# Idle matmuls at the start, eight transposes moved to the tensor engine, and a new written-out order

## The chip, the cores and the metric

The kernel runs on one core of one Trainium2 chip. The metric is the device time of one execution in microseconds (us). A difference is told against the runs of the kernel before on the same chip.

## The reference

Two computations in a row. First a causal attention with a decay ("forgetting attention"), for 8 batches of 8 heads, 576 positions and 64 channels:

```python
scores = (1 / sqrt(D)) * q @ k.T
cum = cumsum(log(clip(f, 1e-4, 1)))               # per head, along the sequence
scores = where(causal, -1e9, scores + cum[i] - cum[j])
attn = exp(scores - rowmax); attn /= attn.sum()
x = attn @ v                                      # x: 4608 tokens x 512
```

Then a bilinear feed-forward network on the 4608 tokens, with 512 channels and 1536 hidden ones:

```python
out = ((x @ w_a) * (x @ w_b)) @ w_out
```

## The kernel before

**Work units.** Heads are worked on in pairs; a pair of one batch is a unit `t` (0 to 31, four units in a batch). The 576 queries of a unit are five blocks (four of 128 and one of 64). For each unit: q and k are loaded, cast to 16 bits and transposed by the tensor engine (`pe_transpose`, tile psT, L285); the scores are made in groups (`qk_group`, tile sc, L417); VectorE adds the decay and takes the row maximum (`do_max` L514 for batch 0, `do_decay` L540 later); ScalarE takes the exponential into P, a 16-bit tile (tiles PA and PB, L567 and L571); VectorE inverts the sums (L581), GpSimd scales P (`do_norm`, L589); P is transposed; the tensor engine multiplies it with v (`do_pv` L631, `do_pv4` L647); VectorE copies the result to xT, the network's input. The network goes through the tokens in pieces of 256, 256, 256, 384 and then 512: 12 steps of psa and psb (`ff_mm`, L914, four matmuls each), a copy by ScalarE (L240), a product by VectorE (L925, tile ht), and pso (L934).

**How P is transposed.** Blocks of P are parts: A0 (six 128x128 blocks, query blocks 0 and 1), A1 (six, query block 2), both joined as A from batch 2 (counting from 0) on, and B (thirteen). For batch 0 (`PEP`) the tensor engine transposes P (`pe_tr`, tile psP, L609) and VectorE or ScalarE copies the result from PSUM (`pe_tr_evict`). For all others SP issues a DMA transpose (`do_tr`). In batches 0 and 1 the transposed A0 and A1 lie in the upper half of xT's storage, so the profile names that transfer xT<-PA. Batches are counted from 1 in the change's own words: its "batch 2" holds the units 4 to 7.

**The decay.** f is loaded, clipped, its logarithm taken on ScalarE and summed up by a scan on VectorE (L187); its high and low 16-bit parts are the tile crow. For batch 0 the decay comes to the scores by extra matmuls on crow; for the units 4 to 7 (`PSPREAD`) it is spread over the rows by a matmul (`spread_mm`, tile scd, L482).

**Weights.** GpSimd issues the loads of w_a and w_b (two row halves, each in a first part of 512 columns and a second part of 1024) and of w_out (L392). Step 0 of the network needs both row halves of the first parts.

**What sets the order.** Every step is an `Op` with a planned engine, duration and dependencies. The planner is not in the file: its result is, as the list `ORDER` of Op numbers, and the string `CHOICE`, which gives the engine of each Op that may run on more than one. The kernel emits the Ops in that order, so each engine's queue, the DMA issues of SP and those of GpSimd among them, is fixed by it. An engine works its queue in order: an instruction that waits holds all those behind it. PSUM and SBUF tiles come from rings (two sc, one pv, three ff).

Of the kernel before, what the change touches and what calls it, by code (L numbers as in the profile page):

```python
# [9 lines left out]
FP32 = mybir.dt.float32  # L10
# [15 lines left out]
def kernel(  # L26
# [11 lines left out]
    nc = tc.nc  # L38
# [32 lines left out]

    def constants():
        make_identity(nc, ident16)
# [130 lines left out]
    o_c = Op("POOL", 4.5, lambda _: constants(), prio=-300)  # L204
# [99 lines left out]
    PEP = tuple(range(1))  # L304

# [372 lines left out]
    def attention(t, base):  # L678
# [12 lines left out]
        if not direct:  # L691
            if t in PSPREAD:
# [340 lines left out]
    for n in cuts:  # L1033
# [3 lines left out]
        0 1 26 20 32 38 3-6 27 28 11 7 2 29 30 12 21 22 8 10 9 13 14 19 33 34 23 24 31 25 18 61 64 35 70 106 15  # L1037
# [7 lines left out]
        178 1739 173 256 174 1741-1743 272 1740 1744 275 265 266 179 273 1745 104 139 276 289 283 282 290 105  # L1045
# [3 lines left out]
        1762-1764 280 287 60 288 221 222 226 484 264 328 385 329 293 150 330 294 472 473 231 1765 334 1766 384  # L1049
        378 339 232 373 1767 1768 379 386 233 194 1769 1771 389 390 340 388 387 485 295 234 1770 1773 341 1774  # L1050
        342 391 392 1775 336 195 1772 1776 274 296 297 393 303 304 474 1777-1779 239 298 475 299 305 1780 338
# [4 lines left out]
        1802 427-429 439 440 435 1804 313 1805 1807 1806 1809 1808 1810 314 424 434 1811 442 441 1812 1813  # L1056
# [4 lines left out]
        528 519-521 529 546 1837 545 413 414 552 1838 530-532 553 547 507 533 514 513 579 676 1786 458 671 460  # L1061
# [6 lines left out]
        608 616 594 636 617-619 614 643 644 620 637 610 684 622 609 596 621 615 1893-1896 638 645 639 646 1898  # L1068
# [10 lines left out]
        1969-1971 798 895 896 816 897 797 1972 787 788 811 794 821 822 1973 823 1974 838 1976 1978 892 836 791  # L1079
        826 827 846 847 818 1975 1977 824 828-830 907 898 903 953 848 854 856 1979 849 1980 842 839 1982 812 806  # L1080
        831 819 813 908 820 832 825 853 855 841 860 917 1983 1981 844 867 861 857 1984 1985 868 837 1986 840 850
        852 899 904 858 1987-1989 863 834 833 1990 1992 843 910 1994 869 954 905 1991 862 1996 1993 918 926 872
# [5 lines left out]
        986 955 980 987 982 1000 984 990 991 1100 992 993 951 952 2023 2018 1002 2026 2029-2031 1003 1006 2034  # L1088
        975 988 2032 1102 983 1010 1005 989 1108 1109 976 994 996 977 1055 1011 1024 1025 1017 2027 1012 2036
        2038 1013 2035 1026 1019 1018 968 2037 1027 1020 2039 969 1008 2040 1007 1031 1028 1032 2041-2043 1033  # L1090
# [50 lines left out]
        2420 2419 2422 2421 2417 2423 2424 2427 2425 2428 2426 2368 2429 2432 2430 2433-2435 2431 2437 2436 2438  # L1141
# [49 lines left out]
```

## Time and profile before

| | us |
|---|---|
| median of 3 runs | 415.94 (415.08 to 416.61) |
| profiled execution | 413.75 |
| its span (first to last instruction) | 412.0 |
| TensorE (PE) busy in it | 388.2 (94%) |
| VectorE (DVE) busy | 302.8 (73%) |
| ScalarE (ACT) busy | 277.8 (67%) |
| GpSimd (POOL) busy | 265.1 (64%) |

Times in the views are us from the start of the span unless marked ns. PE rows are matmuls; PEld are its weight loads, which overlap them. "idle before" is time in which the engine had nothing running ahead of the row, with what released it. A row of several pipelined matmuls gives the time from the first start to the last end; from the starts of two following rows one reads what the first really took of the queue. The tensor engine's granted clock stands in the views as a share of full speed.

### The profile page before, as it was taken

Reading aid. Unit: us, or ns where it says so; the run is one execution under the profiler, and the core shown is the slowest. Engines: PE = TensorE matmul, PEld = TensorE weight load, DVE = VectorE, ACT = ScalarE, POOL = GpSimd, SP = SyncE. Lnnn points to the kernel's source line nnn. Section 1 sums busy time; section 2 is a strip of 40 time slices with the busy share of each in tenths; the row PEclk is TensorE's granted clock in tenths of the full one; section 3 lists DMA queues with packets and bytes.
Section 4 is the critical chain, followed back from the end, with each engine's and each line's share of the span. In section 5 each row is a group of like instructions: output and inputs, shape, how many; then the busy total and the mean of one; then the engine's idle time right before and its main releaser. Section 6 shows DMA issues by size and latency. Waiting matters only on the chain. (4 is left out here: it accounts for less than half of the span.)

```text
span 412.0 us, 10863 instructions
## 1 busy us (share of the span) xinstructions
PE 388.2 (94%) x3788; PEld 209.6 (51%) x3788; DVE 302.8 (73%) x1011; ACT 277.8 (67%) x788; POOL 265.1 (64%) x490
## 2 busy tenths in 40 slices
PE   1698999999999999899999999999999999999995
PEld 1456675756756544444445444444454444444552
DVE  5987998897889859777798789768878793432331
ACT  2877898885987668876786778777877673231230
POOL 6899797877796786875967787767865845000000
PEclk9999999999999999999999999999999999999999
DMA  6999999999999999999999999996996729200102
GB/s 245 200 240 215 227 197 244 211 230 256 257 215 233 288 218 246 221 240 244 232 208 283 298 190 211 266 223 210 186 222 205 156 56 180 84 1 11 68 0 103
DMA packets 153575, 80.56 MB, mean 196 GB/s; under 512 B 130736, under 2 KB 133552, under 8 KB 153520
## 3 DMA queue, kind: packets, MB, share of 16 engines
q1 hardware_dynamic: 149616, 75.02, 78.5%
q0 software_dynamic: 3760, 4.72, 7.0%
q8 instruction: 29, 0.48, 0.5%
q14 instruction: 26, 0.21, 0.2%
q10 hardware_dynamic: 144, 0.13, 0.1%
HBM read 52.05 MB, written 9.58 MB: 150 GB/s over the span
## 5 line engine op out<-in xcount | busy, mean ns | idle before, releaser
L540 DVE CUSTOM_DVE_ANT_0 S<-sc,spread 64x576 f32<-64x576 f32 (+4 forms) x232 | 126.4, 562 | 13.3 <-PE sc L417 6.1
L914 PE MATMUL psa<-xT,wa 128*128 128x512 f16 (+2 forms) x528 | 115.3, 341 | 1.3 <-ACT a L240 0.8
L914 PE MATMUL psb<-xT,wb 128*128 128x512 f16 (+2 forms) x528 | 115.3, 341 | 0.4 <-DVE PTB L244 0.2
L240 ACT CAST a<-psa 128x512 f16<-128x512 f32 (+2 forms) x132 | 66.5, 505 | 57.2 <-PE psa L914 50.5
L925 DVE TENSOR_TENSOR ht<-psb,a 128x512 f16<-128x512 f32 (+2 forms) x132 | 77.4, 590 | 34.2 <-PE psb L914 26.3
L589 POOL TENSOR_SCALAR PA<-PA,st 128x256 f16<-128x256 f16 (+2 forms) x192 | 90.3, 480 | 18.3 <-DVE st L581 12.3
L934 PE MATMUL pso<-wout,ht 128*128 128x512 f16 x432 | 100.0, 380 | 0.0
L571 ACT ACTIVATE PA<-S,st 128x256 f16<-128x256 f32 (+2 forms) x168 | 84.6, 506 | 8.1 <-DVE st L540 8.1
L589 POOL TENSOR_SCALAR PB<-PB,st 128x512 f16<-128x512 f16 (+1 forms) x96 | 67.6, 712 | 24.3 <-DVE st L581 13.1
L914 PEld LDWEIGHTS <-wa 128*128 128x128 f16 x528 | 49.0, 98 | 42.1 <-issue 4.4
L914 PEld LDWEIGHTS <-wb 128*128 128x128 f16 x528 | 49.1, 98 | 40.2 <-issue 1.8
L934 PEld LDWEIGHTS <-ht 128*128 128x128 f16 x432 | 39.8, 98 | 45.6 <-issue 0.9
L571 ACT ACTIVATE PB<-S,st 128x512 f16<-128x512 f32 x56 | 40.4, 721 | 11.1 <-DVE st L540 9.7
L417 PE MATMUL sc<-kT,qT 64*128 64x128 f16 (+4 forms) x384 | 35.8, 274 | 3.1 <-ACT kT L240 1.4
L240 ACT COPY osb<-pso 128x512 f32<-128x512 f32 (+1 forms) x19 | 10.8, 569 | 32.3 <-DMA out_dram<-osb 15.7
L571 ACT ACTIVATION_READ_ACCUMULATOR PA<-S,st 128x1 f32 x168 | 32.3, 192 | 0.0
L244 DVE CAST xT<-pv 128x512 f16<-128x512 f32 (+1 forms) x40 | 23.1, 576 | 6.6 <-PE pv L631 6.4
L244 DVE COPY osb<-pso 128x512 f32<-128x512 f32 (+1 forms) x18 | 12.1, 674 | 20.8 <-PE pso L934 14.9
L631 PEld LDWEIGHTS <-nv 128*64 128x64 f16 x640 | 19.5, 110 | 13.1 <-issue 9.8
L581 DVE RECIPROCAL st<-st 128x2 f32<-128x2 f32 x128 | 18.9, 157 | 9.9 <-ACT PB L571 5.2
L417 PEld LDWEIGHTS <-qT 64*128 64x128 f16 (+1 forms) x384 | 13.8, 96 | 23.0 <-issue 15.6
L567 ACT ACTIVATE PB<-S,st 128x576 f16<-128x576 f32 x28 | 21.7, 775 | 4.4 <-issue 2.3
(92 smaller groups left out, 454.2 us busy)
## 6 DMA issues: line engine op xcount, KB each, us to landing
spread<-cum_d SPq DMA_DIRECT2D x24, 576.0 KB, 5.6
out_dram<-osb SPq DMA_DIRECT2D x35, 256.0 KB, 2.8
q<-in_q_dram SPq DMA_DIRECT2D x15, 576.0 KB, 6.4
k<-in_k_dram SPq DMA_DIRECT2D x15, 576.0 KB, 5.9
v<-in_v_dram SPq DMA_DIRECT2D x32, 256.0 KB, 5.7
wout<-in_moe_w_out_dram POOLq DMA_DIRECT2D x3, 512.0 KB, 7.8
v<-in_v_dram SPq DMA_DIRECT2D x8, 128.0 KB, 4.4
wa<-in_moe_w_a_dram POOLq DMA_DIRECT2D x2, 512.0 KB, 10.3
```

The lines of the kernel that those rows point to most:

```text
L240: nc.scalar.copy(out=out_, in_=in_)
L244: VEC[e].tensor_copy(out=out_, in_=in_)
L417: nc.tensor.matmul(out=dst, lhsT=lhsT, rhs=rhs, start=start, stop=stop, skip_group_check=True)
L540: nc.vector.tensor_tensor_reduce(out=o, in0=x, in1=y, scale=-1.0, scalar=3e38, op0=ADD, op1=MIN, accum_out=m)
L567: nc.scalar.activation(out=p_blocks(t, 4), in_=T[("s" if direct else "z", t, 4)], func=EXP, bias=st[:, 8:9], scale=sign, accum_out=st[:, 1 ...
L571: nc.scalar.activation(out=p_blocks(t, i)[:, :, h, :], in_=(T[("s", t, i)][:, h, :] if direct else T[("z", t, i)][:, h * n:h * n + n]).rea ...
L581: nc.vector.reciprocal(out=st[:, 20 + 2 * i:22 + 2 * i], in_=st[:, 10 + 2 * i:12 + 2 * i])
L589: VEC[e].tensor_scalar(out=p, in0=p, scalar1=st[:, c:c + 1], scalar2=1.0, op0=MUL, op1=MUL)
L631: nc.tensor.matmul(out=o[HP[h], 128 * i:128 * i + 128], lhsT=vt[:, j, pr + NP * h, :], rhs=pt[:, base_blk[i] + 2 * block_at(t, i, j) + h, ...
L914: nc.tensor.matmul(out=p[:, 0:n], lhsT=w16[:, db, 128 * fb:128 * fb + 128], rhs=xTflat[db][:, t0:t0 + n], start=(db == 0), stop=(db == 3))
L925: nc.vector.tensor_tensor(out=ht[:, 0:n], in0=T.pop(("psb", t0, fb))[:, 0:n], in1=T.pop(("a16", t0, fb))[:, 0:n], op=MUL)
L934: nc.tensor.matmul(out=o, lhsT=T[("ht", t0, fb)][:, 128 * tb:128 * tb + 128], rhs=wout16[:, fb, :], start=(fb == 0), stop=(fb == 11))
```

## The change

**Idle matmuls.** `make_identity` becomes an Op of its own, first on GpSimd. Twenty-four Ops `wake0` to `wake23` on the tensor engine each issue two matmuls of 128 rows and 512 columns on the identity (the moving operand is one column of it, broadcast); nobody reads their result, which lies in the ring pv. In the new order four of these Ops (eight matmuls) stand ahead of the first transposition of q, nineteen more stand among the work up to the network's first psa, and one behind it.

**P of the units 4 to 7.** Parts A0 and A1 go the way of batch 0: 48 matmul transposes in eight groups of six, eight copies out of PSUM (five on VectorE, three on ScalarE by the new `CHOICE`), and eight DMA transposes fewer. The part B of these units stays with the DMA.

**New order.** `ORDER` and `CHOICE` are replaced. At the start SP now issues the first loads of q and k ahead of those of f; q of batch 0 is cast by ScalarE in place of VectorE; the first half of w_b whose load stands last is issued behind more of GpSimd's work.

The two lines under `if t in MASKP` make nothing new: `MASKP` starts at unit 8 and `PSPREAD` ends at 7.

```diff
-    def constants():
+    def identity():
         make_identity(nc, ident16)
+
+    def wake(n):
+        x = ps.tile([128, 512], FP32, tag="pv", bufs=1, name="wake")
+        for _ in range(n):
+            nc.tensor.matmul(out=x, lhsT=ident16, rhs=ident16[:, 0:1].to_broadcast([128, 512]),
+                             start=True, stop=True, skip_group_check=True)
+
+    def constants():
         for x in pickh:
...
-    o_c = Op("POOL", 4.5, lambda _: constants(), prio=-300)
+    o_i = Op("POOL", 1.2, lambda _: identity(), prio=-301, name="ident")
+    o_c = Op("POOL", 3.3, lambda _: constants(), [o_i], prio=-300, name="const")
+    for n in range(24):
+        o = Op("PE", 0.427, lambda _: wake(2), [o_i], prio=-290, mode="full", name=f"wake{n}")
+        o.prev = [last_wake] if n else []
+        last_wake = o
+        take(o, "pv")
...
     PEP = tuple(range(1))
+    PEQ = {(t, x) for t in range(4, 8) for x in ("A0", "A1")}
...
+                if t in MASKP:
+                    mc = Op("POOL", 0.9, lambda _: mask_copy(t), list(bcs), prio=prio(0) - 4, name=f"mc{t}")
+                    ml = Op("POOL", 0.42, lambda _: mask_last(t), [mc], prio=prio(3) - 0.5, name=f"ml{t}")
+                    bcu.extend([mc, ml])
...
-            if b in PEP:
+            if b in PEP or (t, part) in PEQ:
                 cuts = {"A": [(0, 6), (6, 12)], "A0": [(0, 6)], "A1": [(6, 12)], "B": [(0, 8), (8, 13)]}[part]
...
     ORDER = """
-        0 1 26 20 32 38 3-6 27 28 11 7 2 29 30 12 21 22 8 10 9 13 14 19 33 34 23 24 31 25 18 61 64 35 70 106 15
...
+        2 51 45 0 1 57 63 28 29 52 53 46 47 30 36 3-7 54 8 9 44 55 48 10 56 31 37 49 50 43 58 59 32 33 35 38
...
     CHOICE = """
-        DDPPDDAADDADAPDAPPDDPPPDDAADDDADDDDADDAAAAAADADDADDDDAAAAADADAAAAAAAADADDADAAAAAAADAADADADAAAADADAAA AAA
+        PDPPDDAAAAAAAAADDPPADPDPDDDADDDADDDADADDAAAAAADADADADADADADDDAADAADAAAAAAAADAAADDAAAADDAAAAADDAAAAA
+        AAAAAAAADAD
```

More of the change, by code (lines that the diff above doesn't have):

```diff
@@ L70 @@
     warm = perm.tile([128, 1], FP32, tag="warm", name="warm")
+    def identity():
+        make_identity(nc, ident16)
+    def wake(n):
[3 more added lines that the diff above has]
+                             start=True, stop=True, skip_group_check=True)
     def constants():
-        make_identity(nc, ident16)
         for x in pickh:
@@ L1100 @@
-        1176-1178 1180 1181 1169 1182 1188 1310 1189 1184 1191 1183 1158 1185 1159 1134 2093 2094 1172 2095 1190
-        1195 1196 1192 2097 1303-1305 1168 1160 1171 2098 1313 2091 1255 1197 1165 1140 1186 1200 2099 2100 1201
-        1193 1116 1202-1204 1206 2102 2104 1212 1216 2106 2103 1220 1228 1198 1199 2108 2107 2110 1222 1221 1223
-        2111 2105 1234 1235 1227 1205 1179 1194 1318 1162 1161 1327 2112 1213 2114 2113 1215 2109 1187 1319 1229
-        1237 1236 2115-2117 1238 1314 1219 1214 2118 2119 1218 1207 1208 1315 1217 2120 1241 1242 1256 1211 2121
@@ L1135 @@
-        1674 1673 2291 2292 1723 1721 1724 2293 2296-2298 2301 1675 2294 1676 2295 2290 2299 2302 1725 2303 1726
-        1677 1678 2304 2305 2300 2306-2308 2310 2309 2311 2312 2314 2316 2313 2315 2317-2320 1727 2322 2321
-        2323 2324 2326 2325 2327 2328 1728 2330 2329 2331 2332 2334 2336 2333 2335 2338 2340 2337 2339 2341 2342
-        2344 2343 2345-2348 2350 2349 2351-2356 2359-2362 2357 2363 2358 2364-2366 2369 2370 2367 2371-2374 2376
-        2375 2378 2377 2380 2379 2382 2381 2384 2383 2386 2388 2387 2385 2389 2390 2392 2391 2394 2393 2396 2395
@@ L1140 @@
-        2398 2397 2400 2399 2402 2401 2404 2403 2406 2405 2408 2407 2410 2409 2412 2411 2414 2413 2416 2415 2418
-        2420 2419 2422 2421 2417 2423 2424 2427 2425 2428 2426 2368 2429 2432 2430 2433-2435 2431 2437 2436 2438
+        2 51 45 0 1 57 63 28 29 52 53 46 47 30 36 3-7 54 8 9 44 55 48 10 56 31 37 49 50 43 58 59 32 33 35 38
[6 rows of a table added]
+        79 275 26 1762 121 1763 1764 27 1766 158 1765 122 153-155 278 276 1768 159 116 82 156 195 196 81 157 150
+        279 1770 1771 1767 160 239 1769 241 151 178 123 124 209 1772 127 166 197 198 210 203 290 277 161 291 240
@@ new lines @@
+        167 199 204 297 280 282 298 1773 128 300 314 281 1774-1776 301 302 315 1777 200 201 307 205 308 1778 164
+        129 1779 303 130 304 165 285 316 309 287 286 223 168 172 1780 242 202 206 169 310 211 1782 288 1781 212
+        311 173 317 243 244 1784 318 248 84 83 313 306 85 1786 1783 1785 1787 249 217 349 1788 213 352 245 218
+        401 354 214 1789 404 1790-1792 1794 254 360 250 411 353 1793 406 174 1796 1795 412 359 175 405 1797 255
+        305 247 312 333 334 320 251 355 1798 407 1799 361 408 1800 1801 505 517 319 246 256-258 356 259 506 413
[5 rows of a table added]
@@ new lines @@
+        337 524 1814 427 1829 428 342 514-516 453 454 1830 1832 343 429 1831 456 338 434 463 339 435 470 1833
[8 rows of a table added]
+        600 1891 1892 603 1893 597 1894 1896 1895 605 604 1897 623 1898-1900 630 1901 601 1902 1904 616 606 1903
+        607 588 589 602 582 590 596 625 1905 711 617 619 1906 624 637 608 609 496 712 713 1907 626 706-708 1877
+        658 721 716 497 638 631 633 498 1908 621 1910 499 618 1909 1911 1912 1914 632 1915 1913 1916 1918 1920
+        640 639 1919 610 611 730 1872 714 644 1917 645 722 614 717 668 659 1922 1923 646 620 661 1924 641 1921
@@ new lines @@
+        634 649 1926 647 1925 627 650-652 669 653 676 648 635 654 655 636 628 629 642 1927 1928 665 718 1929 671
[9 rows of a table added]
+        807 836 1995 829 818 847 791-793 799 1988 924 921 922 837 923 843 826 1996 1999 1997 842 2000 848 828
[7 rows of a table added]
+        912 913 2047 979 2044 978 975 962 963 1042 987 964 2046 980 2048-2050 997-999 1005 976 971 957 970 1130
+        2052 1126 993 990 1011 981 1000 1001 1004 1006 1127 1002 983 992 1012 991 2053 2054 995 2057 1007 1014
+        1128 1013 1134 1998 1032 2055 1018 1019 2058 982 1135 988 1015 1016 1033 1131 994 1132 1020 1023-1026
@@ new lines @@
+        2059 2062 1035 1133 1039 2063 2064 1043 1045 1027 1057 1058 1044 1050 1051 1008 984 985 2067 1041 1036
+        1046 1052 1053 1059 2068 2051 2056 1078 1136 2065 1003 1021 1064 1054 1065 1038 2060 2069 2071 1060 2070
+        1017 1010 1028 1088 1022 1029 1034 2072-2074 1040 1069 1070 1047 1061 1079 1009 1066 1067 2075 2077 1081
+        1037 1085 2079 1146 1137 2066 1141 1071 2076 2078 2080 1072 2081-2083 1089 1103 1062 1048 1030 1031 1150
+        1148 1196 2061 1096 1097 1147 1055 1063 1049 2084-2086 1104 1090 1091 2087 2089 1098 1099 2088 1092 1105
@@ new lines @@
+        2091 1087 2092 2093 2095 1106 2096 1100 2090 1110 1111 2094 1073 1056 1068 1080 1074 1075 1077 1082 1086
+        1138-1140 1115 2097 2098 1093 1149 1142 1160 1151 1112 1113 2099 2101 1117 2100 1084 1116 1083 2102 1118
[3 rows of a table added]
+        1207 2118 1209 1152 1172 1208 1215 1210 2120 2121 1340 1181 1185 1187-1189 1252 1214 1155 1335 2122 2123
[7 rows of a table added]
+        1299-1302 1313 1306 1307 2162 1303 1344 1356 1259 1285 1266 1278 1284 1314 1304 1358 1345 1359 1361 2163
[3 rows of a table added]
+        1378 1385 1386 1330 1331 1545 2185 1387 1381 1374 1388 1369 2188-2190 2186 1392 1380 1365 1393 1389 2191
@@ new lines @@
+        1394 1333 2187 2193 1368 1407 1362 1395 1397 1375 1550 1390 1376 1416 1409 1398 1417 1546 2194 2195 1547
+        1400 1399 1548 2196 1419 1413 1410 2192 2198-2200 1418 1425 1401 1431 1432 1382 1411 2201 1424 1384 1420
[12 rows of a table added]
+        1610 1611 1587 1612 1613 2266 2267 1625 1620 2268 2264 1630 1621 1622 1599 1601 1634-1637 2271-2273
+        1648 1649 1605 2269 1623 1618 1600 1593 1624 2275 1650 1653 2276 1641 1643 2277 2279 2274 1654 1642 2278
+        1656 2281 1712 2265 2270 1567 1672 1586 1606 1615 1663 1594 1614 1644 2280 2282 1655 1657 1651 1652 1658
@@ new lines @@
+        1665 1669 2283 2284 1673 1680 2285 2286 1645 1687 1688 1631 2287-2289 1675 1689 2291 2292 1690 1646 1659
[4 rows of a table added]
+        1745 2318 1741 1746 1686 1705 1692 1698 1678 1735 1685 1704 1714 1729 1742 1728 1749 1743 1736 1750-1752
+        1717 1753 1747 2321 2322 1706 1707 2324 2325 1754 1755 1748 1756 1757 2326 2329-2331 2334 1708 2327 1709
+        2323 2328 2332 2335 1758 2336 1759 2337 2333 2338-2355 2357 2359 2356 2358 2360-2366 1760 2367 2369 2371
+        2368 2370 2372 2373 2375 2374 2377 1761 2379 2376 2381 2380 2383 2378 2384 2385 2387 2388 2386 2382 2389
@@ L1142 @@
+        2392 2393 1710 1711 2394 2397 2390 2398 2399 2402 2403 2395 2391 2396 2400 2404-2406 2401 2407 2409 2408
+        2411 2410 2413 2412 2415 2414 2417 2416 2419 2421 2420 2418 2422 2423 2425 2424 2427 2426 2429 2428 2431
+        2430 2433 2432 2435 2434 2437 2436 2439 2438 2441 2440 2443 2442 2445 2444 2447 2446 2449 2448 2451 2453
+        2452 2455 2450 2454 2456 2457 2460 2458 2461 2459 2462 2465 2463 2466-2468 2464 2470 2469 2471
     """
     CHOICE = """
-        DDPPDDAADDADAPDAPPDDPPPDDAADDDADDDDADDAAAAAADADDADDDDAAAAADADAAAAAAAADADDADAAAAAAADAADADADAAAADADAAA AAA
+        PDPPDDAAAAAAAADDPPADPDPDDDADDDADDDADADDAAAAAADADADADADADADDDAADAAAADAAAAAAAADAAADDAAAADDAAAAADDAAAAA
```

19 lines of the change are left out of this document (removed), and 137 rows, old and new, of the table ORDER.

## The prediction

> **What bounds the kernel now.** I read the windows first, cut at the network's first matmul (34.2 us), then the tensor engine's own waits behind that cut, then the chain of waits.
>
> ```profile
> core 0: us, PE busy (x) PEld busy (x) DVE busy (x) ACT busy (x) POOL busy (x), PEclk, DMA share, GB/s
> 0.00:34.20 34.20, 21.26 (x300) 13.38 (x300) 26.43 (x60) 23.33 (x71) 29.01 (x74) 1.00 0.94 230
> 34.20:150.70 116.50, 112.06 (x1417) 72.69 (x1411) 100.45 (x369) 92.58 (x277) 93.26 (x159) 1.00 1.10 231
> 150.70:350.00 199.30, 196.93 (x1759) 95.04 (x1756) 156.21 (x550) 146.38 (x412) 142.81 (x259) 1.00 0.94 215
> ```
> ```profile
> PE pv L631 <- DMA xT<-PA: 1.4, 3, 0.8
> ```
>
> From 34.2 to 350 us the tensor engine is idle for 4.4 + 2.4 = 6.8 us only, and behind that the chain of waits has nothing but its matmuls until the last output; this stage is bound by its work. A microsecond of work added there is a microsecond of span, and all that waiting can give back is 6.8 us, of which 1.4 us is the wait for the DMA transposes that the change removes. Ahead of 34.2 us the engine is idle for 12.9 us and its matmuls are slow, as two rows of the same 512-column shape show:
>
> ```profile
> 20.82 0.61 PE L482 MATMUL scd<-crow,pick 128*128 128x512 f16 x1
> ...
> 27.53 0.61 PE L482 MATMUL scd<-crow,pick 128*128 128x512 f16 x1
> ...
> 30.85 0.39 PE L482 MATMUL scd<-crow,pick 128*128 128x512 f16 x1
> ...
> 314.92 0.86 PE psa L914 x4
> ```
>
> The same matmul takes 0.61 us until 27.5 and 0.39 at 30.9. Four 512-column matmuls take 0.86 us of the queue late in the run, so one takes 0.215; with 0.61 - 0.39 = 0.22 us more it takes about 0.43: half speed until about 28 us. (The windows give a granted clock of 1.00 there; the durations decide.)
>
> **The start.** Before, the first transposition of q waits for the load that SP issues third, behind the two of f:
>
> ```profile
> 0.81 1.65 SPq L172 DMA_DIRECT2D cum_f<-in_f_dram  x2
> 2.51 0.45 SPq L270 DMA_DIRECT2D q<-in_q_dram  x1
> ...
> 6.28 1.33 DVE L242 TENSOR_SCALAR q<-q 128x512 f16<-128x512 f32 x2 [1.32 <-DMA q<-in_q_dram]
> ...
> 6.87 0.39 PE L285 MATMUL psT<-ident,q 64*128 64x64 f16 x8 [6.87 <-DVE q L242]
> ...
> 11.49 0.51 PE L417 MATMUL sc<-kT,qT 64*128 64x256 f16 x4 [1.41 <-ACT kT L240]
> ```
>
> With q and k issued 1.7 us earlier and f about 1 us later (two issues of some 0.5 us ahead of it), q is cast at 4.6 by ScalarE, and the sums of f are no longer held up by VectorE's 1.33 us on q. I count the first scores at about 9.7 in place of 11.5.
>
> ```profile
> 1.09 0.29 POOL masks.py:199 TENSOR_SCALAR_AFFINE_SELECT ident<-ident 128x128 f16<-128x128 f16 x1
> ```
>
> Eight idle matmuls stand ahead of that transposition: 8 x 0.43 = 3.4 us at half speed, from about 1.5 (the identity is written by 1.38) to 4.9, ahead of q's cast at 5.9. They cost nothing while q lands that late. What raises the clock is not in these rows except by contrast: from 15.7 to 27.5 us the engine was busy almost without a gap, mostly with matmuls of 64 rows, and stayed slow; the rise came after 23 us, where matmuls of 128 rows (psP, pv, scd) take most of the queue. Idle matmuls of 128 rows should raise it within a few us. The Trainium skill (TensorE: Matmul & The Clock Gate, Part 1) says that about 3.4 us of sustained busy time raise it; by that, before would have been fast by about 20 us, which its rows at 20.82 and 27.53 contradict, so time alone isn't the rule here; by the page, a clock that stays low (below, among the rivals) has no chance, by the contrast of the rows it keeps a small one.
>
> With a fast clock, 23 idle Ops take 46 x 0.215 = 9.9 us, the real work ahead of the first psa about 21.26 less half of what ran slow (some 15.5 us ahead of 28.1): 13.5 us. From 5.9 on that is some 21.7 us of queue (the first eight being over). The tensor engine is thus not the limit before about 28 us; the others are. Counted from the two orders, VectorE does 2.6 us less ahead of the first psa (two casts of q 1.33, two spreads 1.36, one transposition copy 0.75 and a low part 0.42 go; a cast of v 0.7 and a P copy 0.55 come), GpSimd some 5 us less, ScalarE 3 us more (it was busy 23.3 of 34.2). VectorE was busy in 21.3 of the 24 us from 10.2 on:
>
> ```profile
> 0.00:10.00 10.00, 1.60 (x36) 1.10 (x37) 5.11 (x12) 2.91 (x5) 6.80 (x34) 1.00 0.68 243
> ```
>
> (26.43 less 5.11.) Less 2.6 that is 18.7; with a tenth of idle time it ends at 10.2 + 20.6 = 30.8. So the first psa comes at about 31, with 29 as the bound without any idle time, against 34.24: **-3.2 us**.
>
> **The weights of step 0.** psb needs both halves of w_b's first part.
>
> ```profile
> 34.24 0.61 PE L914 MATMUL psa<-xT,wa 128*128 128x256 f16 x4
> ...
> 35.13 0.60 PE L914 MATMUL psb<-xT,wb 128*128 128x256 f16 x4
> ```
> ```profile
> 20.57 0.63 POOL L392 DMA_DIRECT2D wb<-in_moe_w_b_dram  x1
> 21.21 1.98 POOL L589 TENSOR_SCALAR PA<-PA,st 128x256 f16<-128x256 f16 x5
> ...
> 25.71 1.13 POOL L244 CAST k<-k 128x1152 f16<-128x1152 f32 x1
> ```
> ```profile
> DMA to landing us min/median/max: 13.8/13.8/13.8
> DMA to landing us min/median/max: 5.7/9.4/13.8
> DMA to landing us min/median/max: 9.0/10.9/11.5
> ```
>
> The last three rows are the times to landing of the load issued at 20.57, of w_b's four loads and of w_a's four. Before, the later half is issued at 20.57 and lands at 34.4. In the new order twelve more scalings of P (0.40 each, by the row of five) and a cast of k (1.1) stand ahead of that issue, 5.9 us, while GpSimd starts on its scalings about 1.2 us sooner: issued at about 25.3. It lands at 31.0 by the shortest, 34.7 by w_b's median and 39.1 by the longest. psb, 0.9 us behind psa, asks for it at 32. The new order issues fewer loads of batch 1 between 20 and 30 us, so I take 33, between the shortest and the median: **+1.0 us** of the gain is lost again; bounds 0 and +7.
>
> **The transposes of P.**
>
> ```profile
> 22.98 0.82 PE L609 MATMUL psP<-ident,PA 128*128 128x128 f16 x6
> ...
> 55.12 0.50 PE L609 MATMUL psP<-ident,PA 128*128 128x128 f16 x6
> 55.46 0.60 PE L914 MATMUL psb<-xT,wb 128*128 128x256 f16 x4
> ```
>
> A group of six takes 0.34 us of the queue where the next work is ready (55.12 to 55.46), and up to its whole 0.50 us where it isn't. Eight groups are 2.7 to 4.0; I take 0.40 each: **+3.2 us**, all behind the first psa, where the engine is the bound. With the slow clock of 22.98 a group took 0.32 us longer; eight that run so would add 2.6 us. The Trainium skill (the same page, Part 4) says that the full clock doesn't engage for transposes; by that, the group of 55.12 should be as slow as that of 22.98, which it isn't.
>
> The eight copies take 5 x 0.55 on VectorE and 3 x 0.80 on ScalarE:
>
> ```profile
> L244 DVE COPY xT<-psP 128x768 f16<-128x768 f16 x7 | 3.8, 549 | 0.0
> L240 ACT COPY xT<-psP 128x768 f16<-128x768 f16 x1 | 0.8, 800 | 0.7 <-PE psP L609 0.7
> xT<-PA SPq DMA_TRANSPOSE x8, 3.7
> ```
>
> Both have 14% and more idle time in the window from 34.2 to 150.7, which hides 2.7 and 2.4 us; if a score group waits for its copy instead, it is at most that. The eight DMA transposes (3.7 us to landing each) go, and with them the waits for xT<-PA: **-1.4 us**. They also leave SP's queue, where loads stand behind them:
>
> ```profile
> SPq L603 <- POOL PA L589: 59.6, 17, 9.4
> ```
>
> This can only bring loads forward; I give it nothing. One idle Op stands behind the first psa: 2 x 0.215, **+0.4 us**.
>
> **The rest of the order.** From the network's first step on, both orders hold the same work per piece of tokens but for the above. The 6.8 us of idle time less the 1.4 stay as they are in the forecast; the bounds are none left (-5.4) and, as a new order has other holes, as much again (+5.4).
>
> **The sum.** -3.2 + 1.0 + 3.2 - 1.4 + 0.4 = 0.0 us. On the profiled execution that is 413.75 us again; this lies 2.2 us under the median of the runs shown, so the forecast is the median, **415.9 us**: no change within 0.5% (2.1 us, about what a measurement of this kernel can tell).
>
> **The rivals.**
> - *Faster: the holes close too.* The weights land in time (-1.0), and the new order, freed of DMA transposes in SP's queue, halves the remaining 5.4 us (-2.7): 412.2; with all of them and the first psa at 29, about 407.5. For it: SP's 59.6 us of waits for P. Against it: GpSimd's and VectorE's work is the same, and each is busy in 80% and more of the stage.
> - *Slower: the half of w_b is late.* At step 0's psb the tensor engine stands still, with the scores and transposes of batch 0 and 1 queued behind it. Each us beyond a landing at 33 costs one: 1.7 more at the median landing (417.6), 6.1 at the longest (422.0). It decides from about 35 on, where the whole gain of the start is gone. For it: w_a's four loads took 9.0 us and more; against it: w_b's shortest took 5.7, and the new order lets fewer loads of q, k and v run beside it.
> - *Slower: other holes.* The order has 3 to 5 us more waits behind the first psa: 419 to 421.
> - *The transposes run at the slow pace*, as at 22.98: +2.6, 418.5; it decides from a group time of some 0.65 us on.
> - *The clock isn't raised.* Then 23 idle Ops cost 46 x 0.43 = 20 us, and the work ahead of the first psa some 20 more; from 1.5 us on it would end at 42, not 31: about 427. Against it: nothing but 128-row matmuls stands there for 3.4 us.
>
> **Chances.** No change 0.38; holes close 0.32; w_b late 0.16; other holes 0.08; slow transposes 0.02; clock not raised 0.04. So faster by over 0.5% 0.32, within 0.38, slower 0.30. The range that holds it 8 times in 10 takes the faster rival down to 410.5 and w_b late to nearly its longest, 421.5; the likeliest case's own range is 413.8 to 418.0.
>
> **What would show it.** Right: 512-column matmuls at 0.39 us before 15 us, first scores near 9.7, first psa near 31, psb of step 0 shortly behind with a DMA wait of about 1 us, eight more psP groups at about 0.4 us, no row "pv L631 <- DMA xT<-PA", tensor engine idle between the first psa and the end of about 6 us. Wrong: a first psa later than 33 or before 29, a wait of several us at psb, or idle time behind it that differs from 5.4 by over 2 us.

## The result, and the profile after

The changed kernel takes 409.75 us (median of 4 runs, 408.86 to 410.57); the kernel before took 415.51 us on the same chip. The ratio is 0.985, 95% interval 0.982 to 0.987. Forecast was "no change" at 415.9, range 410.5 to 421.5: the time lies below the range. The profiled execution spans 407.1 us against 412.0.

The windows of the changed kernel, cut at the network's first matmul (now 33.4) and at the same later step as before:

```profile
core 0: us, PE busy (x) PEld busy (x) DVE busy (x) ACT busy (x) POOL busy (x), PEclk, DMA share, GB/s
0.00:33.40 33.40, 28.34 (x347) 13.98 (x348) 26.25 (x56) 26.44 (x76) 28.77 (x73) 1.00 1.00 243
33.40:149.10 115.70, 113.60 (x1461) 76.05 (x1460) 101.88 (x375) 95.69 (x283) 94.53 (x161) 1.00 1.05 224
149.10:350.00 200.90, 200.44 (x1793) 96.75 (x1792) 158.22 (x551) 146.10 (x412) 140.09 (x257) 1.00 0.94 214
```

The first psa came only 0.9 us earlier. Behind it the tensor engine stands idle for 2.1 + 0.5 = 2.6 us, where before had 6.8. Its matmuls rose from 3494 to 3539 in the whole stretch from the first psa to its end, yet its busy time rose by only 0.5 us. The row of before, then that of after:

```profile
34.20:407.90 373.70, 366.89 (x3494) 196.19 (x3488) 275.97 (x951) 254.12 (x717) 236.07 (x417) 1.00 0.86 194
```
```profile
33.40:403.40 370.00, 367.40 (x3539) 199.05 (x3537) 277.41 (x954) 255.72 (x721) 234.62 (x417) 1.00 0.85 191
```

So the added 3.3 us of transposes and of one idle Op are in, and busy time rose by 0.5: some 2.8 us of other matmul time went (366.89 + 3.3 - 367.40); where, is worked out behind the fourth set of runs. The tensor engine's waits behind the first psa, all that the view gives (in us: total, times, longest):

```profile
PE pv L646 <- DMA PTA<-PA: 1.2, 2, 0.7
PE sc L432 <- ACT PB L586: 0.4, 1, 0.4
PE psT L299 <- DVE osb L258: 0.3, 1, 0.3
PE sc L432 <- DVE st L555: 0.2, 1, 0.2
```

Before had ten rows there, the wait for xT<-PA among them. SP stands far less in waits for P's parts A (before: 59.6 us, 17 times):

```profile
SPq L618 <- POOL PA L604: 16.6, 5, 6.0
```

The start, from the tensor engine's timeline (start, duration):

```profile
1.44 3.88 PE L78 MATMUL wake<-ident 128*128 128x512 f16 x8 [1.44 <-POOL pick L83]
...
10.37 0.34 PE L432 MATMUL sc<-kT,qT 64*128 64x256 f16 x4
...
15.01 0.38 PE L497 MATMUL scd<-crow,pick 128*128 128x512 f16 x1
...
33.38 0.60 PE L933 MATMUL psa<-xT,wa 128*128 128x256 f16 x4
...
34.52 0.60 PE L933 MATMUL psb<-xT,wb 128*128 128x256 f16 x4
```

The clock is up by 15 us, as forecast (0.38 for 512 columns; before 0.61 until 27.5), and the first scores come 1.1 us earlier. The first psa hardly does.

### The profile page after: what moved, and what is told of

Its sections match the earlier page's. It is cut to its first block, busy times and chain, and to the rows that moved or that the text cites. A ratio compares the mean times of both kernels' runs of the same rounds, so it can differ in the third digit from the quotient of the medians.

```text
span 407.1 us, 11060 instructions
## 1 busy us (share of the span) xinstructions
PE 395.7 (97%) x3884; PEld 213.0 (52%) x3884; DVE 304.1 (75%) x1010; ACT 282.5 (69%) x798; POOL 263.4 (65%) x489
## 5 line engine op out<-in xcount | busy, mean ns | idle before, releaser
L586 ACT ACTIVATE PA<-S,st 128x256 f16<-128x256 f32 (+2 forms) x168 | 84.3, 504 | 10.3 <-DVE st L555 10.0
L432 PE MATMUL sc<-kT,qT 64*128 64x128 f16 (+4 forms) x384 | 34.0, 266 | 0.9 <-ACT PB L586 0.4
L254 ACT COPY osb<-pso 128x512 f32<-128x512 f32 (+1 forms) x19 | 10.8, 568 | 27.5 <-PE pso L953 15.7
L555 DVE CUSTOM_DVE_ANT_1 S<-sc,spread 128x256 f32<-128x256 f32 x48 | 19.8, 418 | 8.4 <-PE sc L432 2.3
L521 POOL TENSOR_SCALAR_AFFINE_SELECT spread<-spread 128x256 f32<-128x256 f32 x24 | 9.7, 406 | 24.1 <-DVE st L555 24.0
```

What stands on the lines that cost most here:

```text
L254: nc.scalar.copy(out=out_, in_=in_)
L432: nc.tensor.matmul(out=dst, lhsT=lhsT, rhs=rhs, start=start, stop=stop, skip_group_check=True)
L555: nc.vector.tensor_tensor_reduce(out=o, in0=x, in1=y, scale=-1.0, scalar=3e38, op0=ADD, op1=MIN, accum_out=m)
L586: nc.scalar.activation(out=p_blocks(t, i)[:, :, h, :], in_=(T[("s", t, i)][:, h, :] if direct else T[("z", t, i)][:, h * n:h * n + n]).rea ...
```

## The experiments

The kernels come in four sets. Those of one set share a chip and the runs of before; the medians of before were 416.31, 416.16, 415.71 and 416.18 us. Where idle Ops or transposes go or change their form, their entries leave `ORDER` and `CHOICE` and the numbers shift; such shifted lines are not shown. Theory "order": the gain lies in the order behind the first psa. Rivals: the fast clock of the start, and the DMA transposes that are gone.

### First set: the parts of the change taken away

**new_plain.** The new order with neither idle matmuls nor matmul transposes; each DMA transpose is issued right behind the last scaling that it needs.

```diff
-    for n in range(24):
+    for n in range(0):
...
-    PEQ = {(t, x) for t in range(4, 8) for x in ("A0", "A1")}
+    PEQ = set()
```

> The changed kernel without idle matmuls and with the DMA transposes of units 4 to 7 back, each issued right behind the last scaling it needs: the new order alone. Order (theory: the gain of some 6 us comes from the order behind the first psa, which has 4 us less idle time of the tensor engine and fewer changes between whole-array and half-array matmuls): 409 to 412 us. Clock (rival: the gain is the fast clock from 5 us on): 415 to 418, with the first psa at 35 or later. Transposes (rival: the gain is the DMA transposes that went): 414 to 417.

**new_wake_dma.** The same with the 24 idle Ops kept (of the two edits only `PEQ = set()`).

> The changed kernel with the DMA transposes of units 4 to 7 back, idle matmuls kept. Order: 408 to 411, and as the tensor engine has 2.9 us less work behind the first psa, not slower than the changed kernel unless waits for the transfers (up to 3 us) take its place. Clock: 409 to 411. Transposes: 413 to 417.

**new_peq.** After without any idle matmul (only `range(0)`).

> The changed kernel without any idle matmul. Order: 410 to 412, since the first psa came only 0.9 us earlier with the fast clock. Clock: 415 to 418; 512-column matmuls at 0.6 us until 25 us or later, the first psa behind 35. Transposes: 410 to 412.

**new_wake4_peq.** After with the first four idle Ops (eight matmuls) alone (`range(4)`).

> The changed kernel with the first four idle Ops (eight matmuls) alone; the other forty matmuls are left out. If the eight raise the clock and the real work holds it: clock up at 4.8 us as before, 409 to 410 us, and up to 1 us faster than the changed kernel, since forty matmuls at 0.31 us leave the queue. If the later ones are needed to hold the clock: it falls before 15 us and the time goes towards that without idle matmuls.

| | median, us | ratio (95% interval) |
|---|---|---|
| new_plain | 437.61 | 1.048 (1.043 to 1.053) |
| new_wake_dma | 436.85 | 1.048 (1.042 to 1.053) |
| new_peq | 409.04 | 0.980 (0.975 to 0.985) |
| new_wake4_peq | 408.18 | 0.978 (0.974 to 0.983) |

The idle matmuls bring nothing, and neither does the early fast clock. In new_peq the 512-column matmul is slow until past 21.8 us, as in before, and the first psa comes at 33.78, 0.4 later than in after:

```profile
9.53 0.51 PE L432 MATMUL sc<-kT,qT 64*128 64x256 f16 x4 [1.49 <-ACT kT L254]
...
21.78 0.61 PE L497 MATMUL scd<-crow,pick 128*128 128x512 f16 x1
...
25.93 0.38 PE L497 MATMUL scd<-crow,pick 128*128 128x512 f16 x1
```

The clock rival falls. The DMA transposes, issued so in the new order, cost 28.6 us (new_plain against new_peq). Why shows on SP's queue of new_wake_dma and in the tensor engine's waits behind its first psa:

```profile
SPq L618 <- POOL PA L604: 63.6, 12, 11.6
PE pv L662 <- DMA PTB<-PB: 14.3, 2, 8.5
```
```profile
56.15 16.65 SPq L618 DMA_TRANSPOSE xT<-PA  x3
72.89 0.53 SPq L284 DMA_DIRECT2D k<-in_k_dram  x1
```

Three transposes wait for GpSimd's scaling and hold the load of k behind them for 16.7 us; after issued that k at 55.6. Casts of q and k and the DMA transposes of part B come late in turn: the tensor engine is idle for 25.4 us behind its first psa. Idle time is not all of the loss. Behind a long wait the engine's clock is low again (granted 0.74 from 60 to 80 us and 0.66 from 80 to 100, against 1.00 from 34 to 60), and the same transpositions take half as long again:

```profile
64.44 0.66 PE L299 MATMUL psT<-ident,q 64*128 64x64 f16 x18 [3.56 <-POOL q L256]
...
70.75 0.44 PE L299 MATMUL psT<-ident,q 64*128 64x64 f16 x18
```

But I had put the issues there myself, so this run can't say what the transposes are worth.

### Second set: order, transposes and start apart

**old_peq.** The order of before; the transposes on the tensor engine, where the DMA transposes were issued; no idle matmuls.

The copies out of PSUM stand some six entries behind.

```diff
-    for n in range(24):
+    for n in range(0):
...
     ORDER = """
-        2 51 45 0 1 57 63 28 29 52 53 46 47 30 36 3-7 54 8 9 44 55 48 10 56 31 37 49 50 43 58 59 32 33 35 38
...
+        0 1 27 21 33 39 4-7 28 29 12 8 2 3 30 31 13 22 23 9 11 10 14 15 20 34 35 24 25 32 26 19 62 65 36 71 107
...
```

> The order of before, without idle matmuls; only the transposes of P of batch 2's first blocks (units 4 to 7, both halves) go from the DMA queue to the tensor engine, at the places where the DMA transposes were issued. Theory 'order' (the gain is in the order of the instructions behind the first psa): eight groups add about 2.9 us of matmul time, the 1.4 us wait for xT<-PA goes, so some 1.5 us slower than before, ratio 1.000 to 1.008. Theory 'transposes' (the gain is that the DMA transposes and their waits on SyncE's queue are gone): 5 to 7 us faster, ratio 0.984 to 0.988. In between (0.990 to 0.997): each has a part.

Measured 417.45 us, ratio 1.004 (1.002 to 1.006). Alone, the transposes make the kernel 1.6 us slower by the ratio (0.7 to 2.5); the prediction's terms for them (3.2 - 1.4 = 1.8) lie inside. That they bring the gain by themselves falls.

**hy_newstart** and **hy_oldstart.** Two hybrids, both with matmul transposes and without idle matmuls: hy_newstart has the new order up to the first psa and that of old_peq from there, hy_oldstart the reverse. Against old_peq, hy_newstart is:

```diff
     ORDER = """
-        0 1 27 21 33 39 4-7 28 29 12 8 2 3 30 31 13 22 23 9 11 10 14 15 20 34 35 24 25 32 26 19 62 65 36 71 107
...
+        2 27 21 0 1 33 39 4 5 28 29 22 23 6 12 3 30 20 31 24 32 7 13 25 26 19 34 35 8 9 11 14 10 62 107 36 15 16
...
```

> No idle matmuls, transposes on the tensor engine; the order of after up to the first psa (about 33 us), from there the order of old_peq. Theory 'order behind the first psa': the time of old_peq less at most 0.5 us of the start, ratio 0.998 to 1.007. Theory 'start' (what the start prepares, loads and scores that come earlier, is what is worth the gain): ratio 0.980 to 0.988.

> No idle matmuls, transposes on the tensor engine; the order of before up to the first psa, from there the order of after. Theory 'order behind the first psa': the time of the new order without idle matmuls, plus at most 1 us, ratio 0.980 to 0.988. Theory 'start': no gain, ratio 0.998 to 1.007.

Measured: hy_newstart 418.80, ratio 1.007 (1.005 to 1.009); hy_oldstart 410.80, ratio 0.987 (0.984 to 0.991). The gain goes with the order behind the first psa, given the transposes on the tensor engine. The start alone gives the old body nothing. Windows from first psa to the tensor engine's end: old_peq, hy_newstart, hy_oldstart.

```profile
34.20:412.40 378.20, 370.89 (x3541) 199.37 (x3536) 278.37 (x956) 255.69 (x720) 235.03 (x417) 1.00 0.82 187
```
```profile
33.80:413.00 379.20, 370.56 (x3542) 199.06 (x3536) 277.86 (x956) 255.58 (x720) 235.28 (x418) 1.00 0.82 186
```
```profile
34.20:405.70 371.50, 367.03 (x3541) 198.97 (x3536) 278.22 (x954) 255.84 (x722) 234.63 (x417) 1.00 0.85 191
```

The same 3541 matmuls: idle time falls from 7.3 to 4.5 us (378.20 - 370.89 and 371.50 - 367.03), and busy time by 3.9. Together 6.7 us, the difference of the two medians (6.65).

**new_dma_late.** The new order without idle matmuls, the DMA transposes issued where the matmul transposes stood.

```diff
-    PEQ = {(t, x) for t in range(4, 8) for x in ("A0", "A1")}
+    PEQ = set()
```

In `ORDER` each DMA transpose takes the entry of its matmul transpose; the entries of the eight copies go.

> The new order without idle matmuls, with the DMA transposes of P kept, and issued where the matmul transposes stood in the list, not right behind the last scaling (that placement took 437 us, with SyncE standing 64 us in waits and batch 2's loads behind them). Theory 'order', with the loss of that run from the place of the issues on SyncE's queue: most of the loss goes, 407 to 418 us (ratio 0.98 to 1.005). Theory 'transposes' (the new order needs the transposes on the tensor engine, wherever the DMA is issued): 425 us and more, ratio over 1.02.

Measured 423.20 us, ratio 1.018 (1.014 to 1.021): between the two expectations. The later place gives back 14.4 of the 28.6 us that new_plain was above new_peq, and 14.2 stay (across two sets, so across two chips). The tensor engine's waits behind the first psa show what:

```profile
PE pv L662 <- DMA PTB<-PB: 6.6, 2, 3.8
PE psT L299 <- POOL q L256: 4.0, 1, 4.0
PE pv L646 <- DMA PTA<-PA: 3.2, 2, 2.8
```

DMA transposes of part B and a cast of q, behind SP's queue or GpSimd's, are late. With the DMA transposes at either of these two places the new order loses; an order made for DMA transposes, other than before's, was not tried, so whether it would gain as much stays open.

### Third set: after beside its variants, and the price of a change

**after_again, new_peq_again, new_wake4_again.** The three kernels on one chip.

> The kernel after itself, on the same chip as its two variants without idle matmuls. Theory 'idle matmuls cost a little' (one idle Op stands behind the first psa, 0.44 us, and others in gaps of the start that closed late): 0.5 to 1.5 us slower than the variant without, ratio to before about 0.984. Theory 'they cost nothing': the same within 0.3 us.

> After without any idle matmul, measured beside after. 'Idle matmuls cost a little': 0.980 to 0.982 of before, below after. 'They cost nothing': equal to after. If the early full clock was worth something it would be slower than after by 0.4 us (what the first psa came earlier) or more.

> After with only the first eight idle matmuls (before the first transposes, where the tensor engine has nothing else to do). They lie ahead of all data, so both theories expect the time of the variant without any, within 0.5 us; the fastest of the three by at most that.

Measured 410.59, 408.68 and 409.36 us; ratios 0.986 (0.984 to 0.989), 0.982 (0.980 to 0.985) and 0.985 (0.982 to 0.987). The idle matmuls cost 1 to 2 us by the medians; the intervals overlap, so the size is not settled, but nothing speaks for a gain. In this execution of after the clock rose late, so they ran slow and held the first scores, which come at 12.01, not at 9.53 as in new_peq:

```profile
6.46 2.10 PE L78 MATMUL wake<-ident 128*128 128x512 f16 x4
...
9.09 2.98 PE L78 MATMUL wake<-ident 128*128 128x512 f16 x8
12.01 0.34 PE L432 MATMUL sc<-kT,qT 64*128 64x256 f16 x4
```

Little of that reaches the first psa (33.8, against 33.6 in new_peq_again's profile). Behind it this execution has 4.3 us of idle time against 2.9, with a row that the first profile of after did not have:

```profile
PE psb L933 <- DMA wb<-in_moe_w_b_dram: 1.2, 1, 1.2
```

**switch_probe.** new_wake4_peq with 272 more matmuls of 512 columns on constants ahead of everything. `whole` is one on the whole array; `rows` is a pair on the upper and lower 64 rows, `cols` a pair on the left and right 64 columns.

```diff
+        c = tile("p1whole")
+        for n in range(16):
+            whole(c[:, 0, :])
...
+        c = tile("p5rows")
+        for n in range(16):
+            rows(c)
+        c = tile("p6mixrows")
+        for n in range(16):
+            whole(c[:, 0, :])
+            rows(c)
```

> The variant with eight idle matmuls, with 272 further matmuls on constants ahead of them, in blocks of 16: whole-array alone, into two PSUM banks in turn, accumulating, with other weights each time; pairs of row halves and of column halves alone; and whole ones mixed with such pairs. The time of the kernel is some 50 to 70 us longer and says nothing; the steps within the blocks do. Theory 'changes between whole-array and half-array matmuls cost PE time' (0.96 us against 0.86 for a group of four in front of a half-array one): the mixed blocks take about 0.1 us per round more than the sum of whole ones and pairs alone, so 16 x 0.1 = 1.6 us more. Rival 'the step in front of a half-array matmul is longer for another reason, such as its data': no difference, under 0.02 us a round. The step of 0.31 us of idle matmuls, against 0.215 in psa: it goes to 0.215 to 0.22 in the block that accumulates, or in that with two banks, or in that with other weights, whichever is its cause; in none if it is the constant itself.

Rows of its timeline: a block of 16 whole matmuls, a block of 16 pairs of row halves, and the start of the mixed block.

```profile
10.87 3.65 PE L93 MATMUL p1whole<-ident 128*128 128x512 f16 x16
14.35 3.65 PE L93 MATMUL p2banks<-ident 128*128 128x512 f16 x16
...
24.91 3.66 PE L98 MATMUL p5rows<-ident 64*128 64x512 f16 x32
28.50 0.39 PE L93 MATMUL p6mixrows<-ident 128*128 128x512 f16 x1
28.82 0.39 PE L98 MATMUL p6mixrows<-ident 64*128 64x512 f16 x2
29.14 0.39 PE L93 MATMUL p6mixrows<-ident 128*128 128x512 f16 x1
```

From 10.87 to 14.35, 16 whole matmuls take 3.48 us, 0.218 each; a pair takes as much (24.91 to 28.50 with one change at its end: 3.59, 16 x 0.218 + 0.1). Mixed, each step is 0.322: a round is 0.644, not 0.435. Each change between whole-array and half-array matmuls costs 0.104 us, in both directions; a round holds two, so the expectation named half of it. With column halves a round is 0.66. The last pair of row halves, at 38.49, is followed by a pair of column halves at 38.81: 0.32 there too, so a change from row to column halves costs the same there. In the rival's words the step would be the data's; the data here are all the same constant, so it falls.

The idle matmuls' 0.31 us in after is none of the causes listed: all blocks give 0.218. In after the two matmuls within an idle Op are 0.215 apart, and the next Op starts 0.435 behind the second, which is 0.057 behind its end: each Op waits for the end of the one before. The Ops share the one buffer of the ring pv; that this is why they wait is argued, not tested.

### Fourth set: the price of changes in the kernel, and the start's part

Counted in the trace from group to group, from the change into the first psa on, the tensor engine's queue changes 171 times between whole-array and half-array work in before, 154 in after, 155 in new_peq.

**new_peq_third.** The base: new_peq as above.

> The new order without idle matmuls once more, as the base for the three runs beside it: ratio to before 0.980 to 0.983.

**new_more** and **new_fewer.** new_peq with some entries of `ORDER` moved along the tensor engine's queue, 24 in new_more and ten in new_fewer; the other engines' queues stay. Two such moves of new_fewer (Ops 103 and 142, 144 and 148), and one of new_more (325 and 1764):

```diff
-        57 133 126 255 1746 1747 1743 136 215 1745 217 127 154 99 100 185 1748 103 142 173 174 186 179 266 253
+        57 133 126 255 1746 1747 1743 136 215 1745 217 127 154 99 100 185 1748 142 103 173 174 186 179 266 253
...
-        284 1754 140 105 1755 279 106 280 141 261 292 285 263 262 199 144 148 1756 218 178 182 145 286 187 1758
+        284 1754 140 105 1755 279 106 280 141 261 292 285 263 262 199 148 144 1756 218 178 182 145 286 187 1758
```
```diff
-        264 1757 188 287 149 293 219 220 1760 294 224 60 59 289 282 61 1762 1759 1761 1763 225 193 325 1764 189
+        264 1757 188 287 149 293 219 220 1760 294 224 60 59 289 282 61 1762 1759 1761 1763 225 193 1764 325 189
```

> The same with 24 instructions of the tensor engine behind the first psa each moved past one neighbour on its queue (any place where the move is legal and makes two more changes between whole-array and half-array work): 155 changes become 203, all else stays. Theory 'changes cost 0.104 us each, in the kernel as in the block of constants': 48 x 0.104 = 5.0 us slower than the base, nearly all as busy time, ratio to before 0.992 to 0.996. Rival 'in the kernel they are covered': the base's time within 1 us.

> The same with ten instructions moved by one to three places so that 155 changes become 135. Theory 'changes cost': 20 x 0.104 = 2.1 us less busy time; if the moves open no new waits 2 us faster than the base (ratio 0.975 to 0.978), with waits anything up to 1 us slower, which the idle time would show. Rival 'covered': busy time the same.

**hy_oldstart_again.** The hybrid of the second set, unchanged, beside the base.

> The order of before up to the first psa, then the new one, beside the new order itself. 'The start is worth nothing': the base's time within 1 us. 'Start and body fit each other': 2 to 3 us slower than the base, as the runs of the earlier calls, on other chips, would have it (0.987 against 0.980 to 0.982).

Measured: new_peq_third 408.99 (0.983, 0.979 to 0.987), new_more 415.98 (1.001, 0.998 to 1.004), new_fewer 414.62 (0.996, 0.994 to 0.999), hy_oldstart_again 410.86 (0.987, 0.984 to 0.991). The same windows of new_peq_third, new_more and new_fewer:

```profile
33.90:403.00 369.10, 366.97 (x3542) 198.75 (x3536) 277.75 (x954) 255.93 (x722) 235.95 (x418) 1.00 0.84 191
```
```profile
33.50:410.20 376.70, 371.88 (x3542) 197.58 (x3536) 277.76 (x954) 255.97 (x722) 235.04 (x418) 1.00 0.82 188
```
```profile
33.80:409.40 375.60, 367.50 (x3540) 199.52 (x3536) 277.73 (x954) 255.34 (x722) 234.83 (x418) 1.00 0.81 188
```

new_more: 48 changes more, 4.91 us more of busy time, so "covered" falls; that this is 0.102 for each change, as in the block of constants, turns out below to be luck. The other 2.7 us are idle time (4.8 against 2.1) that moves by a single place opened. new_fewer failed: 20 changes fewer, and busy time is 0.5 higher, not 2.1 lower; idle time is 8.1. Its longest waits (the first was 0.2 in the base, the second not there) fit groups that now stand too early:

```profile
PE sc L432 <- DVE st L555: 2.6, 3, 1.2
PE pv L646 <- DVE xT L258: 1.5, 2, 0.8
```

**Where the busy time went.** The traces of these kernels tell, matmul by matmul. Behind the first psa, take the time from each start to the next and subtract the usual step of its shape (0.216 us for a whole matmul of 512 columns, 0.109 for 256). What is left over falls to changes, to waits, and to short stalls. A wait costs more than its idle time, as two rows of before show:

```profile
72.96 0.60 PE L914 MATMUL psa<-xT,wa 128*128 128x256 f16 x4
74.09 0.35 PE L647 MATMUL pv<-PTB,nv 128*64 128x64 f16 x10 [0.53 <-DVE xT L244]
```

Four matmuls of 256 columns take 0.44 us of the queue, so the next could have started at 73.40. It starts 0.69 later, and the view calls 0.53 of that idle. The other 0.16 is the tail: the last matmul runs on beyond its usual step with nothing behind it, and the view counts that as busy. (Where idle ends and tail begins rests on a modelled end; their sum doesn't.) In us:

| | all matmuls at their usual step | whole/half changes without a wait | waits: number, idle + tail | row/column changes and short stalls |
|---|---|---|---|---|
| before | 341.4 | 161: 15.5 | 21: 6.8 + 3.5 | 6.2 |
| after | 344.4 | 153: 14.7 | 13: 2.6 + 2.1 | 5.9 |
| old_peq | 344.1 | 164: 15.7 | 28: 7.3 + 4.6 | 6.1 |
| hy_oldstart | 343.9 | 152: 14.6 | 13: 4.5 + 2.1 | 6.0 |
| new_peq_third | 343.9 | 153: 14.7 | 12: 2.1 + 2.0 | 6.0 |
| new_more | 344.2 | 191: 18.4 | 24: 4.8 + 3.9 | 5.0 |
| new_fewer | 343.9 | 134: 12.9 | 25: 8.1 + 4.1 | 6.3 |

The first column is the same for the same matmuls, so nothing else is hidden there. A change without a wait costs 0.093 to 0.100 us in the kernel by its kind, between row and column halves too; each wait has a tail of 0.16, whether a change falls in it or not. So new_more's 4.91 us are 3.7 for 38 changes and about 2 for the tails of twelve more waits, less 0.7 elsewhere. And in new_fewer 19 changes fewer did save 1.8 us, but the tails of 13 more waits took 2.1 back. So few changes and few waits have to be found together. hy_oldstart_again lies 1.9 us above the base, with overlapping intervals: of the 7.2 us that the base is under before, the new start may bring up to about 2, with the new body alone.

## Why the prediction was wrong, point by point

- **The start** (-3.2): mis-sized, it was -0.9 (34.24 to 33.38) in the profile and -0.4 in the second one of after. The clock rose as forecast, but the first scores came at 10.37 and the rest did not follow the engine sum: q and k landed late enough that VectorE cast k only at 6.27, and transposes of P waited for GpSimd up to 30.70. I had bounded the first psa by VectorE's busy time alone, and had counted 2.6 us less of it and some 5 us less for GpSimd; ahead of the first psa they were busy for 26.3 and 28.8 us, against 26.4 and 29.0 before. It mattered little: the hybrids give the start at most about 2 us, and only with the new body.

```profile
6.27 1.28 DVE L258 CAST k<-k 128x512 f16<-128x512 f32 x2 [4.01 <-DMA k<-in_k_dram]
```
```profile
30.70 0.51 PE L624 MATMUL psP<-ident,PA 128*128 128x128 f16 x6 [0.49 <-POOL PA L604]
```

- **The weights of step 0** (+1.0): the half of w_b is issued at 26.66 (forecast 25.3). In the first profile psb waits for nothing; in the second it waits 1.2 us. Right in size, though not there each time; the rival of several us did not come.

```profile
26.66 0.65 POOL L407 DMA_DIRECT2D wb<-in_moe_w_b_dram  x1
```

- **The transposes of P** (+3.2 and -1.4): right. The eight groups took 2.9 us of the queue, 0.36 each, and old_peq measured +1.6 for the exchange. Two of the groups also show the change's price: 0.33 us of the queue ahead of psb, 0.43 ahead of half-array scores. The slow pace did not come: none was near 0.82. The Trainium skill (TensorE: Matmul & The Clock Gate, Part 4) would have them without the full clock; the trace disagrees (0.50 for the six), as it did before.

```profile
71.37 0.49 PE L624 MATMUL psP<-ident,PA 128*128 128x128 f16 x6
71.70 0.60 PE L933 MATMUL psb<-xT,wb 128*128 128x256 f16 x4
...
78.11 0.50 PE L624 MATMUL psP<-ident,PA 128*128 128x128 f16 x6
78.54 0.39 PE L432 MATMUL sc<-kT,qT 64*128 64x512 f16 x2
```

- **The idle matmuls** (nothing ahead of the first psa, +0.4 behind it): 0.44 behind it, right. Ahead of it the first psa came 0.4 us earlier with them in one pair of profiles (33.38 against 33.78) and 0.2 later in another (33.8 against 33.6), so nothing is near enough there. The 1 to 2 us by which the medians of after lie higher are not explained by that.
- **The rest of the order** (0, bounds -5.4 to +5.4): this is the step that failed. I let the idle time stay at 5.4, and all matmuls keep their price. Idle time was 2.6 us in the first profile of after and 4.3 in the second, 1.9 to 2.9 in its variants without idle matmuls or with eight. And the other matmuls took 2.8 us less, for which the sum had no term at all: I had no price for what an arrangement does to a matmul's place in the queue. By the table, 1.3 of the 2.8 are tails that went with eight waits, 0.8 are eight changes fewer without a wait (of the 17 fewer in all, eight stood at waits, and one is the change into the first psa), 0.3 are shorter stalls; the remaining 0.4 is not assigned. Waits with their tails fell from 10.3 to 4.7 us: that is the bulk of the gain. Between old_peq and hy_oldstart it is the same: of 3.9 us of busy time 2.5 are tails and 1.1 changes. Which moves of the new list close which wait was not tried.
- **The sum**, with what the first profile measured: -0.9 + 0 + 2.9 + 0.4 - 4.2 (idle, the wait for xT<-PA in it) - 2.8 = -4.6 us; the tensor engine's last matmul ended at 403.4 in place of 407.9. The medians lie 5.8 us apart; what is beyond the 4.6 these two profiles don't explain.
- **The rival "the holes close too"** (412.2) had the right direction, and its size for the holes was right (-2.7 beside the -1.4; measured -4.2 for both), though it had no term for the tails and changes. Its ground, SP's queue freed of DMA transposes, is not enough: old_peq frees it and its idle time is 7.3 us, above before's 6.8. The new list closes the holes, and at the places tried only with the queue freed (new_dma_late: 16.8 us idle).

By the medians two versions lie below after (409.75 and 410.59): without idle matmuls, at 409.04, 408.68 and 408.99 us in three sets, and with the first eight alone, at 408.18 and 409.36. Where they ran beside it, the intervals overlap.

## What to carry to other kernels

Where one engine is busy 98% of a stage and the order of everything is new, don't hold the price of its instructions fixed: count in both orders what depends on the neighbour, here the changes between whole-array and half-array matmuls at 0.1 us each, and give waits a forecast of their own with a width. A wait costs its idle time and a tail that counts as busy, 0.16 us here, so many short waits weigh more than idle time says. Time won at the start isn't won until a run shows that it reaches the end; a hybrid of two orders, cut at one instruction, tells that in two runs. And an order made for one form of an operation can lose far more than the operation's price (14 to 28 us here) when that form is put back.

## What the runs showed of the hardware

- A change between whole-array and half-array matmuls costs 0.104 us each way in a block of constants and 0.093 to 0.100 in the kernel; from row to column halves it costs as much. A pair on two row halves starts together and costs one whole matmul (0.218).
- A wait of the tensor engine costs its idle time and the tail of the matmul ahead of it, 0.16 us (21 waits of before: 6.8 + 3.5 us).
- The clock falls again behind waits: in new_wake_dma, with waits of 3.6, 4.2 and 8.5 us, to a granted 0.74 and 0.66 in the windows that hold them.
- What raises the clock: in switch_probe 12 idle matmuls in a row, 5.1 us from 1.44 on, ran at 0.427 us a step, and the next at 0.22. In after eight, from 1.44, were enough in one execution (rows at 5.45 are fast) and not in another (2.10 us for four at 6.46). In new_wake4_peq the same eight, with transposes and scores behind them, left it slow past 21.79 (0.61):

```profile
1.44 4.24 PE L78 MATMUL wake<-ident 128*128 128x512 f16 x8 [1.44 <-POOL ident masks.py:199]
...
21.79 0.61 PE L497 MATMUL scd<-crow,pick 128*128 128x512 f16 x1
...
25.82 0.38 PE L497 MATMUL scd<-crow,pick 128*128 128x512 f16 x1
```

The Trainium skill (TensorE: Matmul & The Clock Gate, Part 1) has the clock rise after some 3.4 us of sustained busy time, counted in a window that runs freely, so that its onset varies from run to run. Here the onset varies far more than the half microsecond that the page gives: in after it came at about 4.8 us in one execution and at about 10 in the other, both with idle matmuls from 1.44 on and gaps under 0.1 us. The slow time up to 21.8 us in new_wake4_peq does not speak against the page: from 9.5 on it is broken by gaps of 0.2 to 0.8 us, its longest stretch without one is 3.0 us (15.02 to 18.00), and the next, from 20.93 on, brings fast matmuls by 24.7.
